# Weight preparation of two bilinear layers asked for in pieces, one per TensorE step, with six staging buffers in the layers before

## The chip, the cores and the metric

The kernel runs on one core of one Trainium2 chip. The metric is the device time of one execution in microseconds. The kernel before was timed three times: 562.81 us in the median, from 562.11 to 563.57 us.

## The reference

Three blocks follow each other. The attention has 2 batches, 8 heads, 768 positions and 64 values a head; each query sees its neighbours at less than 16 positions and one summary per block of 32 keys. Its 1536 x 512 result goes through a maxout layer and through a bilinear layer:

```python
k_sum = k.reshape(B, H, nb, block, D).max(axis=3)
v_sum = v.reshape(B, H, nb, block, D).mean(axis=3)
...
h = np.maximum(np.maximum(x @ w1, x @ w2), x @ w3)     # 512 -> 768
y = h @ w_out                                          # 768 -> 512
...
a = y @ w_a                                            # 512 -> 1536
b = y @ w_b
out = a * b @ w_out                                    # 1536 -> 512
```

## The kernel before, in words

The 1536 tokens are four chunks of 384, two of each batch. Layers one and two are the maxout block, layers three and four the bilinear one. Every matmul with a weight is done three times, since both operands are split into a rounded part and a residual (`mm3`); results gather in PSUM banks.

**Weights.** 60 tiles of 128 x 512 values come as 64-bit numbers, 512 KB each: 24 for layers one and two, 36 for layers three and four. Each goes through three steps. `w_load` is a DMA of SyncE's queue (L421) into a staging buffer. `w_round` makes a float32 of the 64-bit pattern: a scaling on ScalarE or VectorE (L441 or L439), a second one on ScalarE (L443), a shift and a merge on VectorE (L445, L446) and a sum on GpSimd (L447). `w_split` copies on ScalarE (L451) and subtracts on VectorE or GpSimd (L452) to have the rounded part and the residual; in layers three and four all residuals are VectorE's. Layers three's weights are used as 2 x 2 blocks with seven products in place of eight, so `w_split` of a pair also makes four sums of 128 x 256 on VectorE (L467 to L470), splits these two by two, and splits a remaining half.

**Layers three and four.** The order is a0, b0, a1, o0, b1, a2, o1, ... with six of each. A stage a or b is layer three for one slice of 256 of the 1536 columns: seven products for each of two batches, 14 steps of six matmuls. Their banks are called qd, qb and qg. In the first stage of all and in the last b the steps of one batch come before those of the other; elsewhere they alternate. A stage o is layer four, twelve steps of six matmuls of 128 x 512 into banks called po, with two weights. There are 240 steps. After a step, what empties the bank of the step before is issued (`late`, `flush`): ScalarE keeps copies called s, m and u (L624); VectorE adds a kept copy (L634 for an a result called ca, L640 for a b result called t) or multiplies (L638, the last product, t<-qb,ca). A b result of L640 is multiplied by its ca on GpSimd (L641), and each b result is then split by ScalarE (L514) and VectorE (L515) into hg, the input of layer four. VectorE adds the po banks up (L681).

**What sets the order.** Only SyncE's queue runs as written. On the other engines a scheduler plays the program through with durations of its own and sets each queue's order from that, within the data's dependences; where an instruction is issued inside `issue_after(mark)`, it is not placed ahead of that mark. The main loop over `layers34()` asks `weights(2)` after each step. `weights` issues whole weights: it goes on until the slots of split weights are full (`fits`), and slots come free when a stage ends (`w_freed`), so that the work of several weights is asked for at once at the end of a stage and nothing in between.

**Batch one of the attention.** `keys` (L152) loads key rows and `means` (L173) loads transposed values for each of four head pairs; both take their staging buffer from one pool under the name full1, which has `FB[1]` = 2 buffers. From the row, ScalarE copies (L165) and VectorE takes block maxima (L167) and copies them (L168); from the values, VectorE takes block sums (L183). The staging buffers of layers one and two's weights, after the first eight, are `W64[0]` = 4, and `weights` looks six loads ahead at first and two less later, bounded by these buffers.

The functions that the change touches and what calls them, with the line numbers of the profile:

Of the kernel before, what the change touches and what calls it, by code (L numbers as in the profile page):

```python
# [15 lines left out]
ALU = mybir.AluOpType  # L16
# [26 lines left out]
N1, N2, NK = 3 * FF1 // P, FF1 // P, FF2 // P // 3  # L43
N12, N34 = N1 + N2, 9 * NK
# [8 lines left out]

W64, W32, WBUFS, QB, FB, SM, GB, BANKS = (4, 3), (4, 3), (24, 10), 4, (8, 2), 2, (12, 9), (2, 2, 1, 2, 2)

GATE, ROOM, SUMS, EARLY34 = (2, 3), 16, (46, 48, 50, 52), 6
LEAD, TURN, ERA0, ASKS, AHEAD, PRE, TURNS = 5, (11, 2, 2), 8, (3, 4, 5, 7, 9), (4, 1), 3, ((6, N1 - 6, 6, 4, 4, 8, N1 - 8, 4, 12), (24, 34), (34, 44))

# [10 lines left out]
def attention_then_maxout_then_bilinear(ctx: ExitStack, tc: tile.TileContext, qt, kt, vt, vwin, wall, const, out):  # L77
# [4 lines left out]
    V, A, G, T = nc.vector, nc.scalar, nc.gpsimd, nc.tensor  # L82
# [324 lines left out]
    seq = [*range(N12)] + [part(k, 2 * n + i) for k, n, i in kinds[N12:]]  # L407
# [21 lines left out]
    def w_round(q):  # L429


        r = w64_t.pop(q).bitcast(U32).rearrange("p (n t) -> p n t", t=2)
        lw, hw = r[:, :, 0], r[:, :, 1]
        to = hw.bitcast(F32)
        if q < N12 + EARLY34:

            to = ps_c.tile([P, 512], F32, tag="c", name="psw")
        if BIAS_DVE[era(q)][q % 3]:
            V.tensor_scalar(to, hw.bitcast(F32), 2.0 ** -112, None, ALU.mult)  # L439
        else:  # L440
            A.activation(to, hw.bitcast(F32), AF.Copy, scale=2.0 ** -112)  # L441
        hw = to.bitcast(U32)
        A.activation(lw.bitcast(I32), lw, AF.Copy, scale=2.0 ** -29)  # L443
        w32_t[q] = w = w32_p.tile([P, 512], F32, tag=f"w32{q < N12}", name="w32", bufs=W32[q >= N12])
        V.tensor_scalar(w.bitcast(U32), hw, 3, None, ALU.logical_shift_left)  # L445
        V.scalar_tensor_tensor(w.bitcast(U32), hw, 0x80000000, w.bitcast(U32), ALU.bitwise_and, ALU.bitwise_or)  # L446
        G.tensor_tensor(w.bitcast(I32), w.bitcast(I32), lw.bitcast(I32), ALU.add)  # L447

    def w_parts(r, eng, tag="w34", n=512):
        w = w_p.tile([P, 2, n], F32R, tag=tag, name="wt", bufs=2 if n < 512 else WBUFS[tag != "w"])  # L450
        A.activation(w[:, 0], r, AF.Copy)  # L451
        eng.tensor_tensor(w[:, 1], r, w[:, 0], ALU.subtract)  # L452
        return w

    def w_split(q):
        kind, n, i = kinds[q]
        eng = V if SPLIT_DVE[era(q)][q % 3] else G
        if kind in ("w", "o"):
            w_t[q] = w_parts(w32_t.pop(q), eng, "w" if kind == "w" else "w34")
        elif i == 0:  # L460
            w = w_parts(w32_t[q], eng)
            w_t[kind, n] = {"A11": (w, 0), "A12": (w, 256)}
        else:
            w0, w1 = w32_t.pop(q - 1), w32_t.pop(q)
            (a11, a12), (a21, a22) = ((w[:, 0:256], w[:, 256:512]) for w in (w0, w1))
            s12, s34 = (w32_p.tile([P, 512], F32, tag=f"s{i}", name="s", bufs=1) for i in range(2))
            V.tensor_tensor(s12[:, 0:256], a21, a22, ALU.add)  # L467
            V.tensor_tensor(s12[:, 256:512], s12[:, 0:256], a11, ALU.subtract)
            V.tensor_tensor(s34[:, 0:256], a11, a21, ALU.subtract)
            V.tensor_tensor(s34[:, 256:512], a12, s12[:, 256:512], ALU.subtract)  # L470
            s12, s34, a22 = w_parts(s12, eng), w_parts(s34, eng), w_parts(a22, eng, "wb", 256)
            w_t[kind, n].update(S1=(s12, 0), S2=(s12, 256), S3=(s34, 0), S4=(s34, 256), A22=(a22, 0))

    w_at, w_done, w_freed, w_room = [0, 0, 0], 0, 0, 0

    def fits(n):

        return n <= N12 or n - w_freed <= ROOM and n - max(N12, w_freed) <= WBUFS[1]

    def weights(most):  # L480

        nonlocal w_done, w_room
        for _ in range(most):
            if w_done == len(seq) or not fits(w_room + room[w_done]) or w_done == N12 and not gate:
                return
            w_room += room[w_done]
            w_done += 1
            ahead = min(AHEAD[0] + 2 * (w_done < ERA0 + 4), W64[w_done + AHEAD[0] > N12] - 2 * (w_done >= ERA0 + 4))
            for n, (step, more) in enumerate(((w_load, ahead), (w_round, AHEAD[1]), (w_split, 0))):
                while w_at[n] < min(w_done + more, len(seq) if gate else N12):  # L490
                    step(w_at[n])
                    w_at[n] += 1


    late = []
# [107 lines left out]
    def layer3(kind, n, cs):  # L603

        nonlocal w_freed
        ws = w_t[kind, n]
        ps, kept = {}, {}
        each = [(i, b) for i in range(7) for b in range(B)]
        if (kind, n) in (order34[0], order34[-2]):
            each.sort(key=lambda x: x[1])  # L610
        for i, b in each:
            w, y, bank_ = PRODUCTS[i]
            first = (b, bank_) not in ps
            if first:
                ps[b, bank_] = ps_m.tile([P, 512], F32, tag=f"q{bank_}", name=f"q{bank_}")[:, 0:MAXT * P]
            (wt, o), to = ws[w], ps[b, bank_]
            for k in range(2):
                mm3(to, wt, o + k * P, ops[b, y][:, :, k], first and k == 0, k == 1, not first)
            flush()

            def evac(i=i, b=b, to=to):
                def keep(name):
                    kept[b, name] = t = half(name)
                    A.activation(t, to, AF.Copy)  # L624

                def result(f, j, x):

                    c = 2 * b + j
                    if kind == "a":
                        cs[c, f] = t = half("ca")  # L630
                        if x is None:
                            A.activation(t, to, AF.Copy)
                        else:
                            V.tensor_tensor(t, to, x, ALU.add)  # L634
                        return
                    t = half("t")
                    if x is None:
                        V.tensor_tensor(t, to, cs[c, f], ALU.mult)  # L638
                    else:
                        V.tensor_tensor(t, to, x, ALU.add)  # L640
                        G.tensor_tensor(t, t, cs[c, f], ALU.mult)  # L641
                    gs[n, c, f] = g = hg_p.tile([P, 2, MAXT * P], F32R, tag="g", name="hg", bufs=GB[1])
                    split(g, t, V)

                if i in (0, 1, 2):
                    keep(("s1", "m5", "u2")[i])
                elif i == 3:
                    result(0, 0, kept[b, "s1"])
                elif i == 4:
                    result(1, 1, kept[b, "m5"])  # L650
                elif i == 5:
                    result(0, 1, kept[b, "u2"])
                else:
                    result(1, 0, None)

            late.append(evac)
            yield
        w_freed += 3
# [3 lines left out]
    def layer4(n, q):  # L662
        nonlocal w_freed
        for c in range(NCH):
            for i in range(CHUNKS[c][2]):
                ps = bank("po")
                for f in range(2):
                    w, g = w_t[q + f], gs[n, c, f][:, :, i * P:(i + 1) * P]
                    T.matmul(ps, g[:, 0], w[:, 0], start=(f == 0), stop=False)  # L669
                    T.matmul(ps, g[:, 0], w[:, 1], start=False, stop=False)  # L670
                    T.matmul(ps, g[:, 1], w[:, 0], start=False, stop=(f == 1))  # L671
                flush()

                def evac(c=c, i=i, ps=ps):
                    if n == 0:
                        if not acc:
                            sums = acc_p.tile([P, NCH, MAXT, DM], F32, tag="acc", name="acc", bufs=1)
                            acc.update({(c, i): sums[:, c, i] for c in range(NCH) for i in range(MAXT)})
                        A.activation(acc[c, i], ps, AF.Copy)
                    else:  # L680
                        V.tensor_tensor(acc[c, i], ps, acc[c, i], ALU.add)  # L681
                    if n == NG - 1:
                        r0 = (CHUNKS[c][0] * NT + CHUNKS[c][1] + i) * P
                        nc.sync.dma_start(out=out[r0:r0 + P, :], in_=acc[c, i])

                late.append(evac)
                yield
        w_freed += 2
# [48 lines left out]
            done += 1  # L737
    next(dense[-1], None)
    for _ in layers34():
        weights(2)  # L740
    flush()


# [54 lines left out]
```

## Time and profile before

| what | value |
|---|---|
| median of three runs | 562.81 us (562.11 to 563.57) |
| the profiled execution's own time | 561.15 us |
| its span in the profile | 559.3 us |
| mean granted TensorE clock | 0.998 of full speed |
| TensorE busy | 543.4 us, 97% of the span |
| VectorE busy | 376.6 us, 67% |
| ScalarE busy | 278.0 us, 50% |
| GpSimd busy | 200.8 us, 36% |

The span is what the profiler covers of one execution; the execution's own time is 1.85 us longer. PE is TensorE's matmuls, PEld its weight loads, DVE VectorE, ACT ScalarE, POOL GpSimd, SP SyncE. A matmul's end is modelled: twelve matmuls of a row take 2.24 us together, while the mean of one alone is 336 ns, so that one follows the other after (2.24 - 0.336) / 11 = 0.173 us and a gap shown behind a matmul is 0.16 us shorter than the time that TensorE in fact lost. Rows of VectorE that follow each other without a pause overlap by some 0.07 us (298.80 + 0.54 against 299.27).

### The profile page before, as it was taken

What the parts mean: (1) busy time and instruction counts of PE and PEld (TensorE: products, weight loads), DVE (VectorE), ACT (ScalarE), POOL (GpSimd) and SP (SyncE); (2) the same over time, 40 slices, a digit from 0 to 9 for tenths busy, and PEclk for the clock granted to TensorE, in tenths of its full rate; (3) what the DMA queues carried; (4) which work ended last, traced back from release to release, by engine and by line L of the source; (5) the groups of instructions that cost most, each with busy time, mean ns of one, the idle gap of its engine ahead of it and who ended that gap; (6) DMA issues with size and microseconds to landing.
All of it is one profiled execution on the core that took longest, in us unless ns stands there. A gap on an engine that the chain in (4) does not pass through costs nothing.

```text
span 559.3 us, 9056 instructions
## 1 busy us (share of the span) xinstructions
PE 543.4 (97%) x3374; PEld 513.6 (92%) x3374; DVE 376.6 (67%) x781; ACT 278.0 (50%) x667; POOL 200.8 (36%) x177
## 2 busy tenths in 40 slices
PE   8899999999999999999997999999999999999997
PEld 7889999999999999999997899899899989999985
DVE  5798956964433622839869766866977987773374
ACT  4799765666442413525665656534544453341220
POOL 4389996542110111503604322513413332320030
PEclk9999999999999999999999999999999999999999
DMA  8992473833100020312321222122023120000005
GB/s 315 350 269 84 157 249 119 301 113 111 38 1 2 1 97 16 110 42 76 114 75 39 75 77 76 39 76 79 35 76 114 38 77 37 1 0 1 1 32 194
DMA packets 16987, 51.81 MB, mean 93 GB/s; under 512 B 2096, under 2 KB 2480, under 8 KB 16944
## 3 DMA queue, kind: packets, MB, share of 16 engines
q1 hardware_dynamic: 16944, 51.25, 27.4%
q8 instruction: 26, 0.43, 0.3%
q14 instruction: 17, 0.14, 0.1%
HBM read 48.09 MB, written 3.15 MB: 92 GB/s over the span
## 4 chain that ended last, share of the span: by engine, by line
PE 77%; DVE 12%; DMA 4%; ACT 3%; issue 2%; POOL 2%; SPq 0%; POOLq 0%; DVEq 0%; ACTq 0%
PE ph L511 24%; PE qb L511 13%; PE py L511 9%; PE qg L511 5%; PE po L671 5%; PE po L670 5%; PE po L669 5%; PE qd L511 3%; PE ps L250 3%; DVE wt L452 2%; DVE hg L515 2%; DMA w<-wall 2%; PE psv L305 2%; PE pst L286 1%; DVE t L640 1%
## 5 line engine op out<-in xcount | busy, mean ns | idle before, releaser
L511 PE MATMUL ph<-x,wt 128*128 128x384 f32 x864 | 156.2, 336 | 0.1
L511 PEld LDWEIGHTS ph<-x,wt 128*128 128x128 f32 x864 | 149.2, 188 | 0.7 <-DVE x L515 0.5
L447 POOL TENSOR_TENSOR w<-w,w 128x512 int32<-128x512 int32 x60 | 83.0, 1388 | 154.7 <-DVE w L446 78.0
L511 PE MATMUL qb<-yt,wt 128*128 128x384 f32 x576 | 112.9, 336 | 5.5 <-DVE t L640 2.9
L511 PEld LDWEIGHTS qb<-yt,wt 128*128 128x128 f32 x576 | 101.6, 188 | 10.8 <-DVE t L640 3.3
L514 ACT ACTIVATE hg<-t 128x384 fp32r<-128x384 f32 x72 | 37.0, 522 | 81.2 <-DVE t L538 41.5
L641 POOL TENSOR_TENSOR t<-t,ca 128x384 f32<-128x384 f32 x36 | 42.8, 1201 | 85.4 <-DVE t L640 83.0
L681 DVE TENSOR_TENSOR acc<-po,acc 128x512 f32<-128x512 f32 x60 | 40.8, 686 | 27.5 <-PE po L671 27.4
L511 PE MATMUL qg<-yt,wt 128*128 128x384 f32 x288 | 58.0, 336 | 0.5 <-DVE t L640 0.5
L670 PE MATMUL po<-wt,hg 128*128 128x512 f32 x144 | 56.7, 394 | 0.0
L669 PE MATMUL po<-wt,hg 128*128 128x512 f32 x144 | 56.2, 390 | 0.5 <-ACT hg L514 0.5
L671 PE MATMUL po<-wt,hg 128*128 128x512 f32 x144 | 56.2, 396 | 0.2 <-DVE hg L515 0.2
L511 PE MATMUL py<-hg,wt 128*128 128x384 f32 x288 | 55.2, 340 | 0.0
L511 PEld LDWEIGHTS qg<-yt,wt 128*128 128x128 f32 x288 | 50.6, 188 | 2.8 <-DVE t L640 1.0
L538 DVE TENSOR_TENSOR t<-ph,t 128x384 f32<-128x384 f32 x48 | 26.6, 554 | 37.1 <-PE ph L511 31.1
L511 PEld LDWEIGHTS py<-hg,wt 128*128 128x128 f32 x288 | 49.6, 188 | 0.1
L257 ACT ACTIVATE s<-s,nm 128x120 f32<-128x120 f32 x96 | 37.1, 390 | 22.0 <-DVE nm L256 21.3
L451 ACT ACTIVATE wt<-w 128x512 fp32r<-128x512 f32 (+1 forms) x60 | 35.0, 584 | 18.7 <-PE qb L511 12.8
L452 DVE TENSOR_TENSOR wt<-w,wt 128x512 fp32r<-128x512 f32 (+1 forms) x44 | 32.4, 737 | 16.2 <-ACT wt L451 16.2
L515 DVE TENSOR_TENSOR hg<-t,hg 128x384 fp32r<-128x384 f32 x48 | 40.6, 856 | 3.8 <-ACT hg L514 3.8
L515 POOL TENSOR_TENSOR hg<-t,hg 128x384 fp32r<-128x384 f32 x24 | 26.1, 1091 | 46.7 <-ACT hg L514 45.7
L443 ACT ACTIVATE w<-w 128x512 int32<-128x512 uint32 x60 | 39.3, 668 | 0.5 <-DMA w<-wall 0.5
(80 smaller groups left out, 776.7 us busy)
## 6 DMA issues: line engine op xcount, KB each, us to landing
w<-wall SPq DMA_DIRECT2D x60, 512.0 KB, 3.3
q<-qt SPq DMA_DIRECT2D x15, 384.0 KB, 6.7
row<-kt SPq DMA_DIRECT2D x8, 416.0 KB, 5.8
full<-vt SPq DMA_DIRECT2D x8, 384.0 KB, 6.4
out<-acc SPq DMA_DIRECT2D x12, 256.0 KB, 2.0
v<-vwin SPq DMA_DIRECT2D x12, 192.0 KB, 6.7
v<-vwin SPq DMA_DIRECT2D x12, 96.0 KB, 6.8
q<-qt SPq DMA_DIRECT2D x1, 256.0 KB, 4.4
```

Source lines behind the costliest of these rows:

```text
L257: A.activation(s[:, a], s[:, a], AF.Exp, bias=nm[:, a:a + 1], scale=-1.0, accum_out=sm[:, a:a + 1])
L443: A.activation(lw.bitcast(I32), lw, AF.Copy, scale=2.0 ** -29)
L447: G.tensor_tensor(w.bitcast(I32), w.bitcast(I32), lw.bitcast(I32), ALU.add)
L452: eng.tensor_tensor(w[:, 1], r, w[:, 0], ALU.subtract)
L511: T.matmul(ps, w[:, i, o:o + P], x[:, j], start=first and n == 0, stop=last and n == 2, skip_group_check=more)
L514: A.activation(dst[:, 0], src, AF.Copy)
L515: eng.tensor_tensor(dst[:, 1], src, dst[:, 0], ALU.subtract)
L641: G.tensor_tensor(t, t, cs[c, f], ALU.mult)
L669: T.matmul(ps, g[:, 0], w[:, 0], start=(f == 0), stop=False)
L670: T.matmul(ps, g[:, 0], w[:, 1], start=False, stop=False)
L671: T.matmul(ps, g[:, 1], w[:, 0], start=False, stop=(f == 1))
L681: V.tensor_tensor(acc[c, i], ps, acc[c, i], ALU.add)
```

## The change

Three things change.

1. `w_round` and `w_split` become generators that stop two times in a `w_round`, and one time or, for the second weight of a pair, five times in a `w_split`. `work` runs the three steps of a weight as before, `pieces(n)` goes on by n stops, and `weights` runs a whole weight through `pieces`. The loop over layers three and four asks `pieces(1)` after each step instead of `weights(2)`, and issues it inside `issue_after(mark[0])`. `mark[0]`, which layers one and two's `evac` set, is now set by VectorE's evacuations of layers three and four as well. `made` goes on with pieces where a step needs a weight that is not there yet; its loop never runs here.
2. `w_split` of a pair splits its first two sums before it makes the other two.
3. `W64` goes from (4, 3) to (6, 3), so that loads of layers one and two are asked for six ahead at first and four later, and `FB` goes from (8, 2) to (9, 1): one staging buffer in place of two under the name full1.

```diff
-W64, W32, WBUFS, QB, FB, SM, GB, BANKS = (4, 3), (4, 3), (24, 10), 4, (8, 2), 2, (12, 9), (2, 2, 1, 2, 2)
+W64, W32, WBUFS, QB, FB, SM, GB, BANKS = (6, 3), (4, 3), (24, 10), 4, (9, 1), 2, (12, 9), (2, 2, 1, 2, 2)
...
         V.tensor_scalar(w.bitcast(U32), hw, 3, None, ALU.logical_shift_left)
+        yield
         V.scalar_tensor_tensor(w.bitcast(U32), hw, 0x80000000, w.bitcast(U32), ALU.bitwise_and, ALU.bitwise_or)
         G.tensor_tensor(w.bitcast(I32), w.bitcast(I32), lw.bitcast(I32), ALU.add)
+        yield
...
             V.tensor_tensor(s12[:, 0:256], a21, a22, ALU.add)
             V.tensor_tensor(s12[:, 256:512], s12[:, 0:256], a11, ALU.subtract)
+            yield
+            s1 = w_parts(s12, eng)
+            w_t[kind, n].update(S1=(s1, 0), S2=(s1, 256))
+            yield
             V.tensor_tensor(s34[:, 0:256], a11, a21, ALU.subtract)
             V.tensor_tensor(s34[:, 256:512], a12, s12[:, 256:512], ALU.subtract)
-            s12, s34, a22 = w_parts(s12, eng), w_parts(s34, eng), w_parts(a22, eng, "wb", 256)
-            w_t[kind, n].update(S1=(s12, 0), S2=(s12, 256), S3=(s34, 0), S4=(s34, 256), A22=(a22, 0))
+            yield
+            s3 = w_parts(s34, eng)
+            w_t[kind, n].update(S3=(s3, 0), S4=(s3, 256))
+            yield
+            w_t[kind, n].update(A22=(w_parts(a22, eng, "wb", 256), 0))
+            yield
...
+    def work():
+
+        ahead = min(AHEAD[0] + 2 * (w_done < ERA0 + 4), W64[w_done + AHEAD[0] > N12] - 2 * (w_done >= ERA0 + 4))
+        for n, (step, more) in enumerate(((w_load, ahead), (w_round, AHEAD[1]), (w_split, 0))):
+            while w_at[n] < min(w_done + more, len(seq) if gate else N12):
+                w_at[n] += 1
+                yield from step(w_at[n] - 1) or ()
+
+    begun = [iter(())]
+
+    def pieces(most):
...
+        while most:
+            for _ in begun[0]:
+                most -= 1
+                if not most:
+                    return True
             if w_done == len(seq) or not fits(w_room + room[w_done]) or w_done == N12 and not gate:
-                return
+                return False
             w_room += room[w_done]
             w_done += 1
...
+            begun[0] = work()
...
-                            V.tensor_tensor(t, to, x, ALU.add)
+                            mark[0] = V.tensor_tensor(t, to, x, ALU.add).ins
...
-                        V.tensor_tensor(t, to, x, ALU.add)
+                        mark[0] = V.tensor_tensor(t, to, x, ALU.add).ins
...
-                        V.tensor_tensor(acc[c, i], ps, acc[c, i], ALU.add)
+                        mark[0] = V.tensor_tensor(acc[c, i], ps, acc[c, i], ALU.add).ins
...
     for _ in layers34():
-        weights(2)
+        with tc.issue_after(mark[0]):
+            pieces(PIECES)
```

The instructions are the same in kind and number; their order moves. L640 of before is L675 of the changed kernel, L638 is L673, L452 is L454, L446 is L447, L515 is L550, L467, L469, L468 and L470 are L471, L477, L472 and L478.

VectorE at the end of the stage b0, kernel before: qd, qb and qg are banks that it empties, t the result of b, w and s are weights and sums of weights, wt a split weight, hg the split product. The last row is the evacuation of batch one's first qb bank.

```order
L640 TENSOR_TENSOR t<-qd,s_3375 128x384
L640 TENSOR_TENSOR t<-qb,m_3384 128x384
L452 TENSOR_TENSOR wt<-s,wt 128x512
L467 TENSOR_TENSOR s<-w_3534 128x256
L469 TENSOR_TENSOR s<-w_3511,w_3534 128x256
L468 TENSOR_TENSOR s<-s,w_3511 128x256
L452 TENSOR_TENSOR wt<-w_3511,wt 128x512
L470 TENSOR_TENSOR s<-w_3511,s 128x256
L515 TENSOR_TENSOR hg<-t,hg 128x384
L445 TENSOR_SCALAR w_3663<-w_3659 128x512
L515 TENSOR_TENSOR hg<-t,hg 128x384
L640 TENSOR_TENSOR t<-qb,m_3392 128x384
```

VectorE at the same place in the changed kernel, beginning a few weight instructions earlier; its evacuation of that bank is the last row but two.

```order
L447 SCALAR_TENSOR_TENSOR w_3341<-w_3337,w_3341 128x512
L445 TENSOR_SCALAR w_3379<-w_3375 128x512
L454 TENSOR_TENSOR wt<-w_3015,wt 128x256
L447 SCALAR_TENSOR_TENSOR w_3379<-w_3375,w_3379 128x512
L454 TENSOR_TENSOR wt<-w_3341,wt 128x512
L675 TENSOR_TENSOR t<-qd,s_3361 128x384
L675 TENSOR_TENSOR t<-qb,m_3373 128x384
L550 TENSOR_TENSOR hg<-t,hg 128x384 x2
L675 TENSOR_TENSOR t<-qb,m_3387 128x384
L675 TENSOR_TENSOR t<-qg,u_3397 128x384
L675 TENSOR_TENSOR t<-qg,u_3409 128x384
```

Between the two evacuations t<-qb,m stood nine instructions, seven of them on weights; now two stand there, both of hg.

VectorE directly behind that, kernel before, as far as the second t<-qb,ca, which closes b0 (the first row is again the evacuation of qg).

```order
L640 TENSOR_TENSOR t<-qg,u_3409 128x384
L452 TENSOR_TENSOR wt<-s,wt 128x512
L515 TENSOR_TENSOR hg<-t,hg 128x384
L452 TENSOR_TENSOR wt<-w_3352,wt 128x256
L515 TENSOR_TENSOR hg<-t,hg 128x384
L638 TENSOR_TENSOR t<-qb,ca 128x384
L445 TENSOR_SCALAR w_3686<-w_3682 128x512
L638 TENSOR_TENSOR t<-qb,ca 128x384
```

VectorE at the same place in the changed kernel, as far as the first t<-qb,ca.

```order
L471 TENSOR_TENSOR s<-w_3379 128x256
L477 TENSOR_TENSOR s<-w_3341,w_3379 128x256
L447 SCALAR_TENSOR_TENSOR w_3511<-w_3507,w_3511 128x512
L472 TENSOR_TENSOR s<-s,w_3341 128x256
L550 TENSOR_TENSOR hg<-t,hg 128x384
L454 TENSOR_TENSOR wt<-w_3379,wt 128x256
L550 TENSOR_TENSOR hg<-t,hg 128x384
L478 TENSOR_TENSOR s<-w_3341,s 128x256
L673 TENSOR_TENSOR t<-qb,ca 128x384
```

With the shift (L445) of another weight ahead of the first of these rows, nine instructions stand between the last t<-qg,u and the first t<-qb,ca, seven of them on weights; before there were four, two of them on weights.

TensorE at the end of the stage b3, kernel before: po is layer four of the stage o2, which is mixed in; the rows go from b3's last qb products into a4.

```order
L511 MATMUL qb<-yt,wt 128x384 x12
L511 MATMUL qg<-yt,wt 128x384 x12
L511 MATMUL qb<-yt,wt 128x384 x12
L511 MATMUL qg<-yt,wt 128x384 x6
L669 MATMUL po<-wt,hg 128x512
L670 MATMUL po<-wt,hg 128x512
L669 MATMUL po<-wt,hg 128x512
L670 MATMUL po<-wt,hg 128x512
L511 MATMUL qg<-yt,wt 128x384 x6
L671 MATMUL po<-wt,hg 128x512 x2
```

TensorE at the same place in the changed kernel.

```order
L546 MATMUL qb<-yt,wt 128x384 x12
L546 MATMUL qg<-yt,wt 128x384 x18
L546 MATMUL qb<-yt,wt 128x384 x6
L546 MATMUL qg<-yt,wt 128x384 x6
L546 MATMUL qb<-yt,wt 128x384 x6
L705 MATMUL po<-wt,hg 128x512
L706 MATMUL po<-wt,hg 128x512
L705 MATMUL po<-wt,hg 128x512
L706 MATMUL po<-wt,hg 128x512
L707 MATMUL po<-wt,hg 128x512 x2
```

Six matmuls of qg of the next stage now stand ahead of its first qb: the step that needs the qb bank, emptied by t<-qb,ca, comes six matmuls later, and the two qb steps are apart.

On SyncE's queue, two loads of weights that stood between the loads of batch one's head pairs now stand ahead of the first of them, 15 in a row in place of 13.

## Rows read from the trace of the kernel before

**Rows 1.** The page's first lines: the span, and TensorE's and the other engines' busy time.

```profile
span 559.3 us, 9056 instructions
PE 543.4 (97%) x3374; PEld 513.6 (92%) x3374; DVE 376.6 (67%) x781; ACT 278.0 (50%) x667; POOL 200.8 (36%) x177
```

**Rows 2.** Busy time of each engine by window: start:end, length, then busy (instructions), clock, DMA.

```profile
70.00:280.00 210.00, 210.00 (x1407) 206.89 (x1407) 120.28 (x274) 102.20 (x253) 74.18 (x62) 1.00 0.28 93
300.00:310.00 10.00, 7.04 (x39) 6.36 (x38) 10.00 (x15) 6.88 (x14) 6.62 (x6) 1.00 0.15 54
```

**Rows 3.** TensorE's waits from 285 to 559 us: total us, times, longest us.

```profile
PE qb L511 <- DVE t L640: 2.9, 1, 2.9
PE qb L511 <- DVE t L638: 2.0, 4, 0.9
PE qb L511 <- ACT u L624: 0.6, 1, 0.6
PE qg L511 <- DVE t L640: 0.5, 1, 0.5
PE po L669 <- ACT hg L514: 0.5, 1, 0.5
PE po L671 <- DVE hg L515: 0.2, 1, 0.2
```

**Rows 4.** TensorE's timeline at b0's end: start us, us, what [idle before <-releaser].

```profile
301.01 2.24 PE L511 MATMUL qb<-yt,wt 128*128 128x384 f32 x12
306.20 1.33 PE L511 MATMUL qb<-yt,wt 128*128 128x384 f32 x6 [2.95 <-DVE t L640]
307.37 4.63 PE L511 MATMUL qg<-yt,wt 128*128 128x384 f32 x24
312.94 2.35 PE L511 MATMUL qb<-yt,wt 128*128 128x384 f32 x12 [0.95 <-DVE t L638]
```

**Rows 5.** VectorE's timeline at the same place.

```profile
298.80 0.54 DVE L640 TENSOR_TENSOR t<-qd,s 128x384 f32<-128x384 f32 x1
299.27 0.54 DVE L640 TENSOR_TENSOR t<-qb,m 128x384 f32<-128x384 f32 x1
...
305.60 0.55 DVE L640 TENSOR_TENSOR t<-qb,m 128x384 f32<-128x384 f32 x1
...
306.53 1.25 DVE L446 SCALAR_TENSOR_TENSOR w<-w,w 128x512 uint32<-128x512 uint32 x1
...
311.88 0.54 DVE L515 TENSOR_TENSOR hg<-t,hg 128x384 fp32r<-128x384 f32 x1
...
313.61 0.68 DVE L446 SCALAR_TENSOR_TENSOR w<-w,w 128x512 uint32<-128x512 uint32 x1
```

**Rows 6.** VectorE's sums of line 469: minimum/median/maximum ns of one, first and last start.

```profile
L469 DVE TENSOR_TENSOR s<-w,w x12: 411/418/1243, 229.8 to 472.1; 128x256 f32<-128x256 f32 x12
```

**Rows 7.** The page's costliest groups: count | busy, mean ns of one | idle before.

```profile
L447 POOL TENSOR_TENSOR w<-w,w 128x512 int32<-128x512 int32 x60 | 83.0, 1388 | 154.7 <-DVE w L446 78.0
...
L514 ACT ACTIVATE hg<-t 128x384 fp32r<-128x384 f32 x72 | 37.0, 522 | 81.2 <-DVE t L538 41.5
L641 POOL TENSOR_TENSOR t<-t,ca 128x384 f32<-128x384 f32 x36 | 42.8, 1201 | 85.4 <-DVE t L640 83.0
...
L451 ACT ACTIVATE wt<-w 128x512 fp32r<-128x512 f32 (+1 forms) x60 | 35.0, 584 | 18.7 <-PE qb L511 12.8
```

**Rows 8.** TensorE's waits from 40 to 72 us.

```profile
PEld ph L511 <- DVE x L515: 0.5, 1, 0.5
```

**Rows 9.** SyncE's queue, the second row of batch one.

```profile
98.59 0.33 SPq L152 DMA_DIRECT2D row<-kt  x1
```

**Rows 10.** VectorE's timeline where batch one's rows are consumed.

```profile
98.38 0.94 DVE L183 TENSOR_REDUCE mean<-full 128x24 f32<-128x768 f32 x1
...
101.85 0.95 DVE L167 TENSOR_REDUCE top<-row 128x24 f32<-128x768 f32 x1 [0.51 <-DMA row<-kt]
```

**Rows 11.** VectorE's waits from 285 to 540 us.

```profile
DVE wt L452 <- ACT wt L451: 20.4, 13, 3.7
```

More of the change, by code (lines that the diff above doesn't have):

```diff
@@ L52 @@
             ("S4", "B22", "g"), ("A22", "T4", "b"))
-W64, W32, WBUFS, QB, FB, SM, GB, BANKS = (4, 3), (4, 3), (24, 10), 4, (8, 2), 2, (12, 9), (2, 2, 1, 2, 2)
+W64, W32, WBUFS, QB, FB, SM, GB, BANKS = (6, 3), (4, 3), (24, 10), 4, (9, 1), 2, (12, 9), (2, 2, 1, 2, 2)
 GATE, ROOM, SUMS, EARLY34 = (2, 3), 16, (46, 48, 50, 52), 6
-LEAD, TURN, ERA0, ASKS, AHEAD, PRE, TURNS = 5, (11, 2, 2), 8, (3, 4, 5, 7, 9), (4, 1), 3, ((6, N1 - 6, 6, 4, 4, 8, N1 - 8, 4, 12), (24, 34), (34, 44))
+PIECES, LEAD, TURN, ERA0, ASKS, AHEAD, PRE, TURNS = 1, 5, (11, 2, 2), 8, (3, 4, 5, 7, 9), (4, 1), 3, ((6, N1 - 6, 6, 4, 4, 8, N1 - 8, 4, 12), (24, 34), (34, 44))
 EARLY, BIAS_DVE, SPLIT_DVE = 16, ((0, 1, 0), (0, 1, 0), (0, 0, 0)), ((0, 0, 1), (0, 0, 1), (1, 1, 1))
@@ L468, in w_split @@
             V.tensor_tensor(s12[:, 256:512], s12[:, 0:256], a11, ALU.subtract)
+            yield
+            s1 = w_parts(s12, eng)
+            w_t[kind, n].update(S1=(s1, 0), S2=(s1, 256))
+            yield
             V.tensor_tensor(s34[:, 0:256], a11, a21, ALU.subtract)
             V.tensor_tensor(s34[:, 256:512], a12, s12[:, 256:512], ALU.subtract)
-            s12, s34, a22 = w_parts(s12, eng), w_parts(s34, eng), w_parts(a22, eng, "wb", 256)
-            w_t[kind, n].update(S1=(s12, 0), S2=(s12, 256), S3=(s34, 0), S4=(s34, 256), A22=(a22, 0))
+            yield
+            s3 = w_parts(s34, eng)
+            w_t[kind, n].update(S3=(s3, 0), S4=(s3, 256))
+            yield
+            w_t[kind, n].update(A22=(w_parts(a22, eng, "wb", 256), 0))
+            yield
     w_at, w_done, w_freed, w_room = [0, 0, 0], 0, 0, 0
@@ L478, in fits, with weights, made @@
         return n <= N12 or n - w_freed <= ROOM and n - max(N12, w_freed) <= WBUFS[1]
-    def weights(most):
-        nonlocal w_done, w_room
-        for _ in range(most):
+    def work():
[6 more added lines that the diff above has]
+    def pieces(most):
+        nonlocal w_done, w_room
+        while most:
[3 more added lines that the diff above has]
+                    return True
             if w_done == len(seq) or not fits(w_room + room[w_done]) or w_done == N12 and not gate:
-                return
+                return False
             w_room += room[w_done]
             w_done += 1
[L488 to L492, printed above, removed]
+            begun[0] = work()
+    def weights(most):
+        for _ in range(most):
+            if not pieces(1):
+                return
+            for _ in begun[0]:
+                pass
+    def made(kind, n, tile_):
+        while not (tile_ in w_t.get((kind, n), ()) if kind in "ab" else n in w_t):
+            assert pieces(1)
     late = []
@@ L605, in layer3 @@
         nonlocal w_freed
-        ws = w_t[kind, n]
         ps, kept = {}, {}
@@ L615, in layer3 @@
                 ps[b, bank_] = ps_m.tile([P, 512], F32, tag=f"q{bank_}", name=f"q{bank_}")[:, 0:MAXT * P]
-            (wt, o), to = ws[w], ps[b, bank_]
+            made(kind, n, w)
+            (wt, o), to = w_t[kind, n][w], ps[b, bank_]
             for k in range(2):
@@ L667, in layer4 @@
                 for f in range(2):
+                    made("o", q + f, None)
                     w, g = w_t[q + f], gs[n, c, f][:, :, i * P:(i + 1) * P]
```

## The prediction

> **What bounds the kernel now.** The page's first lines come first: TensorE is busy for 543.4 of 559.3 us [rows 1]. The windows come second. From 70 to 280 us, layers one and two, it has 210.00 us of work in 210 [rows 2]: nothing can be won there, only lost. What the change can win lies in layers three and four, and so TensorE's waits from 285 to 559 us are the third view. They are few: 2.9 us for t<-qb,m (L640), 2.0 us in four waits for t<-qb,ca (L638), 0.6 us for a copy of ScalarE, 0.5 us for L640 again, 0.5 and 0.2 us for hg [rows 3]. That is 6.7 us, and all but the 0.6 hang on VectorE or on the split of hg.
>
> The fourth view is the place of the longest wait, at the end of b0. Between 300 and 310 us VectorE is busy for 10.00 of 10 us and TensorE for 7.04 [rows 2]. TensorE's last qb products before the gap end at 303.25 (301.01 + 2.24), and it goes on at 306.20 [rows 4]; VectorE empties that bank at 305.60 [rows 5]. VectorE could have done so from 303.25 on, 2.35 us sooner, had it not been working through nine queued instructions that follow the evacuation at 299.27, seven of them on weights of later stages. The second wait, 0.95 us at 312.94 [rows 4], is the same thing one step on.
>
> **The change part by part.** Counts and kinds of instructions stay, so the sum is one of waits. It is made on the profiled execution, 561.15 us (its span of 559.3 and 1.85 us around it); the median shown is 562.81, 1.66 us more, and the forecast is moved by that.
>
> *A, the wait of 2.95 us.* In the changed order only two hg subtractions stand between the two t<-qb,m. They need a product of GpSimd and a copy of ScalarE each. t<-qd ends at 299.34 [rows 5]; two products of 1.20 us and a copy of 0.52 [rows 7] give 302.3, and the second subtraction of 0.54 [rows 5] is done by some 302.9, ahead of 303.25. The evacuation is then late only by its own length: 2.95 becomes 0.6, -2.35 us. If the bank were free ahead of the products, 0.4 more; if two GpSimd sums of weights (1.388 us each [rows 7]) stood ahead of the two products, the hg would be done at 305.7, a loss of 0.3. Bounds -2.75 and +0.3; I take -2.35, since the row's times put the hg ahead of the bank.
>
> *B, the wait of 0.95 us for t<-qb,ca.* The weight work has to go somewhere, and here it is: nine instructions now stand between the last t<-qg,u and t<-qb,ca where four stood. From the moment when t<-qb,m lets TensorE go on, TensorE has 30 matmuls, at 0.173 us each 5.2 us [rows 4]. VectorE has two evacuations of 0.55, six short weight instructions of 0.42 [rows 6], a merge of 0.68, two hg of 0.54 and the evacuation itself: 1.1 + 2.5 + 0.7 + 1.1 + 0.55 = 5.9, less 0.07 of overlap for each of twelve, 5.1 us. So at best it just fits (-0.95, and 0.16 of modelled end). At worst each of the seven weight instructions is stretched, as L469's longest to 1.24 [rows 6] and the merge to 1.25 [rows 5]: 0.82 x 6 + 0.57 = 5.5 more, a wait of 5.4, +4.5. I take two of the seven stretched, since the median of L469 is 0.418 and only its tail is long: 5.1 + 1.6 - 5.2 = 1.5 us, +0.6.
>
> *C, D, E, the smaller waits.* The 0.2 us for hg goes with A (-0.2; bounds -0.2 and +0.5, the nearest wait for hg). In b1 to b3 there are four waits: t<-qb,ca three times, 1.03 us (2.0 less B's 0.95), and t<-qg,u once, 0.5 [rows 3]. In the changed order more of TensorE's work stands ahead of the qb bank that it waits for, as the six matmuls of qg at b3's end (1.04 us, more than any of the four), and the evacuations of qg follow those of qb directly. I take 1.55 to 0.2, -1.35; bounds -1.55, and +1.0 if one new wait as long as the present 0.95 comes. The 0.5 us for ScalarE's copy of hg late in b5 [rows 3]: the copies of weights are done by then in the changed order, -0.5; bounds -0.5 and 0. The 0.6 us ahead of b0 waits for a copy of ScalarE, which the change does not touch: 0.
>
> *F, modelled ends.* A matmul alone shows 0.336 us but the next can follow after 0.173, so each wait that vanishes gives 0.16 more than its row shows. Four do (C, E and two of D): -0.65.
>
> *G, staging of six.* Two loads of weights come sooner. The one wait behind a late weight is 0.5 us of PEld for x at about 65 us [rows 8], behind a chain that begins with a load: -0.3, bounds -0.5 and 0.
>
> *H, one staging buffer for batch one.* The wait for a buffer stands on SyncE's queue, and behind it the q and v loads of the same head pair and all later ones; VectorE's maxima and, through the scores, TensorE wait for these. Before, the second row is issued at 98.59 [rows 9], as soon as the first row's maximum is done, and the next maximum still waits 0.51 us for it [rows 10]: this load has no slack. In the changed kernel it waits for the sum of the values too, 0.94 us [rows 10]. TensorE has layers one and two to do meanwhile and no gap there [rows 2], so some is covered. Between 0 and 0.9 I take +0.5.
>
> Sum: -2.35 + 0.6 - 0.2 - 1.35 - 0.5 - 0.65 - 0.3 + 0.5 = -4.25. On the profiled execution 561.15 becomes 556.9; on the median 562.81 becomes 558.6.
>
> **A rule that speaks against it.** L469 takes 0.411 us at the least and 1.243 at the most for one shape [rows 6], and the merge 0.68 and 1.25; the evacuations stay at 0.54 or 0.55 [rows 5]. The Trainium skill, page "SBUF — State Buffer", section "Who interferes with whom", says that VectorE and GpSimd share a pair of ports as an exclusive lock, that VectorE instructions with two SBUF inputs are among those held up, and that those with one are not; the trace agrees in these numbers, since the evacuations read one operand from PSUM. By that rule the change puts B's weight instructions beside GpSimd's products by ca, which B's sum prices at two stretched instructions; the rule at its strictest is the first rival.
>
> **The rivals.**
> *R1, the stall moves rather than goes.* Three products of 1.20 us [rows 7] hold VectorE up for 3.6 us in B's stretch instead of 1.6: the wait there is 5.1 + 3.6 - 5.2 = 3.5, +2.55 instead of +0.6, and the same mechanism keeps D's 1.35. -4.25 + 1.95 + 1.35 = -0.95: 561.9. For it speaks that VectorE has no free time in this window [rows 2], against it that L469's median is the short one.
> *R2, the one buffer stalls the attention of batch one.* Each of the seven loads behind the first waits for the consumer of the one before it, 0.94 us each [rows 10]: 6.6 instead of 0.5, 564.7. For it speaks the present wait of 0.51 [rows 10], against it that TensorE is without a gap [rows 2].
> *R3, a queue's head waits: the other side.* A piece per step issues a weight's merge, GpSimd's sum (1.388), ScalarE's copy (0.584) [rows 7] and VectorE's residual a step or two apart. VectorE works in order; in the changed order the residual of w_3341 comes, with 1.3 to 1.5 us of work between, behind a chain of 1.97: it waits some 0.6, and the evacuations t<-qd and t<-qb,m stand right behind it. Ten stages have such a place; if each costs TensorE 0.7 us, that is 7 us: 565.6. It decides from six places on (6 x 0.7 = 4.2). Against it: VectorE already waits 20.4 us in 13 places for the copy L451 [rows 11], one of 3.7 us, and TensorE's waits are still only 6.7 us [rows 3], because it has other work in its queue.
> *R4, nothing.* The order moves but the waits stay what they are: 562.8.
>
> **How the numbers follow.** What a measurement of this kernel can tell from no change is about 0.3%, 1.7 us: below 561.1 is faster, above 564.5 slower. Forecast 0.60 (558.6; its own range 556 to 561, from B at its short end with D at its best to A half kept); R1 0.13, R2 0.08, R3 0.14, R4 0.05. Nearly all of the forecast, and a little of R1, is faster, 0.60; R1's rest, half of R2 and R4 are no change, 0.21; R3 and the other half of R2 are slower, 0.19. The best ends of A to G together give some -7.5, 555.3, the low end; the high end of 564.7 takes in R1, R2 and R4 and leaves R3 out, as the case with the highest price.
>
> **What would show it.** Right: among TensorE's waits from 285 us on the one of 2.9 us for t<-qb,m is under 0.8, one for t<-qb,ca in b0 lies between 0.5 and 2, all together under 4 us; between 300 and 310 us TensorE is busy for over 9 us; from 70 to 280 us it stays at 210. Wrong for A: t<-qb,m still over 2 us late, with GpSimd's sums ahead of its products. R1: t<-qb,ca over 3 us, with L469 and the merge at 1.24 around it. R2: TensorE below 207 us from 70 to 280, VectorE waiting for row or full. R3: new waits of TensorE for L675 or L673 right behind a residual L454 that waits for ScalarE, in six stages or more. The time is off with the steps right if waits come in banks that have none now, the po banks above all, since VectorE's weight work now lies evenly over all steps.

## The result: 566.18 us, 0.68% slower

The changed kernel takes 566.18 us in the median of four runs (565.60 to 567.31), the kernel before 562.70 beside it: a ratio of 1.0068, 95% interval 1.0055 to 1.0081. The forecast was 558.6, the range ended at 564.7. Between the two profiled executions, 561.15 and 566.29 us, the difference is 5.1 us, since that of before is one of its quicker ones; the trace of after accounts for 5.0 of them.

The page of after begins so:

```profile
span 564.5 us, 8995 instructions
PE 545.7 (97%) x3374; PEld 516.5 (91%) x3374; DVE 372.4 (66%) x781; ACT 279.4 (49%) x667; POOL 200.5 (36%) x177
```

TensorE still counts as busy for 97%, with 2.3 us more of it than in [rows 1] for the same matmuls; 1.5 us of that are matmuls that ran slower, as shown below. The same two windows as in [rows 2]:

```profile
70.00:280.00 210.00, 210.00 (x1409) 206.92 (x1408) 116.82 (x269) 102.27 (x254) 73.34 (x61) 1.00 0.25 83
300.00:310.00 10.00, 8.37 (x46) 7.41 (x44) 7.78 (x13) 6.28 (x14) 7.28 (x7) 1.00 0.30 107
```

Layers one and two lose nothing, and b0's end has won: TensorE is busy for 8.37 us where it was 7.04. What has come in its place shows in TensorE's waits from 285 us on (total, times, longest), to be read beside [rows 3]:

```profile
PE qb L546 <- DVE t L673: 5.7, 4, 2.6
PE qg L546 <- ACT m L659: 3.0, 3, 1.6
PE qb L546 <- DVE t L675: 0.7, 1, 0.7
PE qb L546 <- ACT u L659: 0.6, 1, 0.6
```

L675 is L640 of before, L673 is L638, L659 is ScalarE's copies L624. The wait of 2.9 us for t<-qb,m is 0.7, those for hg are gone, but t<-qb,ca takes 5.7 in place of 2.0, and copies called m, which nobody waited for, 3.0.

Counted from one matmul's start to the next, less the usual 0.173 us (0.231 for po), all that TensorE loses from 280 us on is 9.5 us before and 14.5 after, +5.0. By place: the wait for t<-qb,m of b0 3.2 to 1.0; t<-qb,ca of b0 1.2 to 0.7; m in b0 none to 1.9; b1 to b4 2.7 to 9.8; the two waits for hg 1.2 to none. The loss is in b2, b3 and b4; b0 as a whole has won 0.8.

**b4.** TensorE's longest wait, with VectorE and GpSimd at that time (start us, us, what):

```profile
503.67 1.31 PE L546 MATMUL qb<-yt,wt 128*128 128x384 f32 x6 [2.58 <-DVE t L673]
```

```profile
496.28 1.24 DVE L445 TENSOR_SCALAR w<-w 128x512 uint32<-128x512 uint32 x1
497.44 2.11 DVE L447 SCALAR_TENSOR_TENSOR w<-w,w 128x512 uint32<-128x512 uint32 x2
499.46 3.68 DVE L550 TENSOR_TENSOR hg<-t,hg 128x384 fp32r<-128x384 f32 x3
503.07 1.01 DVE L673 TENSOR_TENSOR t<-qb,ca 128x384 f32<-128x384 f32 x2
```

```profile
494.79 3.61 POOL L676 TENSOR_TENSOR t<-t,ca 128x384 f32<-128x384 f32 x3 [1.50 <-DVE t L675]
499.17 3.09 POOL L448 TENSOR_TENSOR w<-w,w 128x512 int32<-128x512 int32 x2 [0.78 <-ACT hg L549]
```

VectorE is never idle here. A shift (L445) and two merges of weights, the pieces of two steps, come ahead of the three hg. Beside GpSimd's three products by ca, which run to 498.40, the shift takes 1.24 us where the median of these shifts is 0.42, and the merges take 2.11 in place of 1.3 (0.68 each in [rows 5], less 0.07 of overlap). The merges release two sums of GpSimd, and beside these the three hg take 3.68 us in place of some 1.5 (0.54 each in [rows 5], less 0.07 of overlap twice). t<-qb,ca waits behind all of it.

**b3.** Here ScalarE is late first, then VectorE.

```profile
449.59 0.40 ACT L453 ACTIVATE wt<-w 128x256 fp32r<-128x256 f32 x1
449.94 0.67 ACT L441 ACTIVATE w<-w 128x512 f32<-128x512 f32 x1
450.51 0.66 ACT L443 ACTIVATE w<-w 128x512 int32<-128x512 uint32 x1
451.06 0.51 ACT L549 ACTIVATE hg<-t 128x384 fp32r<-128x384 f32 x1
451.47 0.48 ACT L659 ACTIVATE m<-qg 128x384 f32<-128x384 f32 x1
```

```profile
452.00 1.34 PE L546 MATMUL qg<-yt,wt 128*128 128x384 f32 x6 [1.59 <-ACT m L659]
454.41 2.29 PE L546 MATMUL qb<-yt,wt 128*128 128x384 f32 x6 [1.07 <-DVE t L673]
```

Three weight instructions stand on ScalarE ahead of m, without a pause. The six matmuls behind 454.41 take 2.29 us, and those at 452.00, just ahead of them, 1.34. The windows around it (length, TensorE busy, ..., granted clock) say why:

```profile
450.00:455.00 5.00, 2.34 (x11) 1.69 (x10) 5.00 (x9) 3.57 (x8) 2.02 (x2) 0.94 0.08 18
455.00:460.00 5.00, 5.00 (x22) 4.87 (x21) 3.62 (x9) 3.50 (x7) 0.00 (x0) 0.72 0.23 90
460.00:465.00 5.00, 5.00 (x29) 4.84 (x28) 3.15 (x6) 1.50 (x3) 1.30 (x1) 1.00 0.27 94
```

After the two waits TensorE is granted the lower of its two levels (1.2 in place of 2.4 GHz) for some 3 us: matmuls follow each other after 0.320 us in place of 0.173, which costs 1.5 us more. That is part of b3's loss, not another cause. In most executions of the kernel before, the mean granted clock is as low as in the changed kernel's (0.994 to 0.997 in 13 of the 17 timed beside mark_all, 0.993 to 0.996 in the changed kernel's four), but 0.998 in the profiled one; between the medians, which lie 3.5 us apart, this part therefore counts for less.

### The profile page after: what moved, and what is told of

Read it like the earlier page. It is cut to its first block, busy times and chain, and to the rows that moved or that the text cites. A ratio compares the mean times of both kernels' runs of the same rounds, so it can differ in the third digit from the quotient of the medians.

```text
span 564.5 us, 8995 instructions
## 1 busy us (share of the span) xinstructions
PE 545.7 (97%) x3374; PEld 516.5 (91%) x3374; DVE 372.4 (66%) x781; ACT 279.4 (49%) x667; POOL 200.5 (36%) x177
## 4 chain that ended last, share of the span: by engine, by line
PE 83%; DVE 8%; DMA 3%; ACT 2%; issue 2%; POOL 1%; SPq 0%; ACTq 0%
PE ph L546 27%; PE qb L546 15%; PE py L546 9%; PE qg L546 6%; PE po L707 5%; PE po L706 5%; PE po L705 5%; PE qd L546 3%; PE ps L250 3%; DVE hg L550 2%; PE psv L305 2%; PE pst L286 2%; DMA full<-vt 1%; DMA q<-qt 1%; DVE w L447 1%
## 5 line engine op out<-in xcount | busy, mean ns | idle before, releaser
L546 PE MATMUL qb<-yt,wt 128*128 128x384 f32 x576 | 116.4, 339 | 7.1 <-DVE t L673 5.7
L546 PE MATMUL qg<-yt,wt 128*128 128x384 f32 x288 | 59.9, 339 | 3.0 <-ACT m L659 3.0
L676 POOL TENSOR_TENSOR t<-t,ca 128x384 f32<-128x384 f32 x36 | 41.0, 1156 | 49.0 <-DVE t L675 44.7
L550 POOL TENSOR_TENSOR hg<-t,hg 128x384 fp32r<-128x384 f32 x24 | 26.6, 1112 | 47.7 <-ACT hg L549 47.7
L550 DVE TENSOR_TENSOR hg<-t,hg 128x384 fp32r<-128x384 f32 x48 | 34.7, 735 | 9.4 <-ACT hg L549 9.2
L275 POOL TENSOR_TENSOR s<-s,r 128x720 f32<-128x720 f32 x16 | 22.3, 1392 | 44.7 <-DVE r L273 32.4
```

The lines of the kernel that those rows point to most:

```text
L546: T.matmul(ps, w[:, i, o:o + P], x[:, j], start=first and n == 0, stop=last and n == 2, skip_group_check=more)
L550: eng.tensor_tensor(dst[:, 1], src, dst[:, 0], ALU.subtract)
```

## The experiments

Each kernel was timed in five rounds beside the kernel before, which took 562.41 to 563.03 us in these groups; the ratios are to that.

### mark_all: the mark at t<-qb,ca too

```diff
-                        V.tensor_tensor(t, to, cs[c, f], ALU.mult)
+                        mark[0] = V.tensor_tensor(t, to, cs[c, f], ALU.mult).ins
```

> The changed kernel, with the mark set by the evacuation t<-qb,ca (L673) too, so that pieces asked for after it are not placed ahead of it. Theory 'place' (in the changed kernel weight pieces stand on VectorE between the last t<-qg,u and t<-qb,ca, and TensorE waits there): TensorE's waits for L673 fall from 5.7 to under 1 us, those for ScalarE's m from 3.0 to under 1, the stretch at half clock behind 454 us is gone, 556 to 560 us. Theory 'port' (VectorE is late there because GpSimd's products and sums hold it up, whatever stands there): the hg subtractions stay beside the products and are late still, 562 to 565 us. Theory 'staging' (the buffers cost the time): no change, 565 to 567 us.

Measured: 559.09 us, ratio 0.9935 (0.9923 to 0.9948). One line turns +0.68% into -0.65%. TensorE's waits from 285 us on:

```profile
PE qb L546 <- ACT u L659: 2.5, 2, 1.9
PE qb L546 <- DVE t L675: 0.7, 1, 0.7
PE qd L546 <- DVE t L675: 0.6, 1, 0.6
PE qb L546 <- ACT s L659: 0.3, 1, 0.3
```

None for L673 and none for m: theory 'place' holds, and 'staging' falls, as staging is that of the changed kernel. The scheduler also ordered TensorE's queue anew (in b3 the last twelve qb matmuls now stand together, with three po matmuls ahead of them), and what that gave by itself is not shown. The expectation missed one thing, a new wait of 1.88 us at 458 us, on ScalarE, with a stretch at the lower clock behind it (granted clock 0.76 from 460 to 465 us):

```profile
456.38 0.67 ACT L441 ACTIVATE w<-w 128x512 f32<-128x512 f32 x1 [2.72 <-DMA w<-wall]
456.95 0.65 ACT L443 ACTIVATE w<-w 128x512 int32<-128x512 uint32 x1
457.50 0.85 ACT L659 ACTIVATE u<-qb 128x384 f32<-128x384 f32 x2
```

```profile
458.02 1.49 PE L546 MATMUL qb<-yt,wt 128*128 128x384 f32 x6 [1.88 <-ACT u L659]
```

The head of ScalarE's queue waits 2.72 us for a weight to land, and the copy u that TensorE needs stands two instructions behind it.

### mark_all_old_staging: the same with W64 (4, 3) and FB (8, 2)

```diff
-W64, W32, WBUFS, QB, FB, SM, GB, BANKS = (6, 3), (4, 3), (24, 10), 4, (9, 1), 2, (12, 9), (2, 2, 1, 2, 2)
+W64, W32, WBUFS, QB, FB, SM, GB, BANKS = (4, 3), (4, 3), (24, 10), 4, (8, 2), 2, (12, 9), (2, 2, 1, 2, 2)
```

> As mark_all, with the staging of the kernel before, W64 (4, 3) and FB (8, 2). Theories 'place' and 'port': within 0.7 us of mark_all, as the order in layers three and four is the same. Theory 'staging': 3 to 5 us under mark_all, and TensorE's waits in layers three and four the same in both.

Measured: 558.45 us, ratio 0.9931 (0.9917 to 0.9944), within the interval of mark_all. The staging buffers, six or four, one or two, are worth nothing that shows.

### no_mark: pieces without the mark

```diff
     for _ in layers34():
-        with tc.issue_after(mark[0]):
-            pieces(PIECES)
+        pieces(PIECES)
```

With the staging of before.

> Pieces one per step, but without the mark around them, and with the staging of the kernel before. In the order the nine instructions, seven on weights, stand between b0's two t<-qb,m again, and two to four ahead of t<-qb,ca. Theory 'place': the wait for t<-qb,m is back at 2 to 3 us, those for t<-qb,ca at 1 to 3 us in all, 561 to 564 us. Rival 'pace' (work spread evenly over the steps costs by itself, through queue heads that wait for GpSimd and ScalarE): 565 to 567 us, as the changed kernel.

Measured: 562.53 us, ratio 1.0007 (0.9997 to 1.0017), no change. The waits are those of [rows 3] again:

```profile
PE qb L546 <- DVE t L675: 3.1, 1, 3.1
PE qb L546 <- DVE t L673: 1.7, 3, 1.2
PE qg L546 <- DVE t L675: 0.9, 1, 0.9
```

So the pieces alone neither win nor lose, and, as the staging is worth nothing, it is the mark that removed b0's long wait. In the changed kernel the mark held weight work behind t<-qb,m and t<-qg,u, and not behind t<-qb,ca: the work that it pushed out came to stand there.

### products_on_dve_b2_on: the products by ca on VectorE

```diff
-                        G.tensor_tensor(t, t, cs[c, f], ALU.mult)
+                        (V if n > 1 else G).tensor_tensor(t, t, cs[c, f], ALU.mult)
```

The rest is the changed kernel.

> The changed kernel with the products by ca of the slices 2 to 5 on VectorE in place of GpSimd; the order up to the end of b1 is unchanged, and ahead of t<-qb,ca stand as many weight instructions as before plus up to three products. Theory 'port': no instruction of VectorE there is stretched any more, TensorE's waits in b2 to b4 (6.9 us in the changed kernel) fall under 2 us, 559 to 562 us. Theory 'place': VectorE's queue ahead of t<-qb,ca is longer than before, the waits stay at 5 us or more, 565 to 569 us.

Measured: 558.49 us, ratio 0.9933 (0.9921 to 0.9945). The waits:

```profile
PE qg L546 <- ACT m L659: 1.9, 2, 1.6
PE qb L546 <- DVE t L673: 1.9, 2, 1.5
PE qb L546 <- DVE t L675: 0.7, 1, 0.7
PE qb L546 <- ACT u L659: 0.6, 1, 0.6
```

From b2 on 6.9 us of waits became about 2 (1.5 for L673 in b2, some 0.4 for m in b3; the rest is b0's, where no product was moved), and the time at the lower clock is gone, though VectorE has more to do. So 'place' as first put is not enough: weight work ahead of t<-qb,ca costs what it does because of what GpSimd has to do beside it. Either cure removes the loss. Not all of the 5 us is shown to be the stretch alone, for three more things moved. The scheduler placed the weight work somewhat differently from b2 on; it ordered TensorE's queue anew (in b4, fifteen more matmuls stand ahead of the last qb steps); and ScalarE's hg copies, two of which wait 1.51 and 0.63 us for products in b3 of the changed kernel and stand ahead of m, no longer depend on GpSimd. The sums of weights stayed on GpSimd, and VectorE is still stretched beside them: its own L471 takes 1.53 us at 401 us, in b2, beside one of GpSimd's that begins at 400.73, ahead of the wait that is left.

### mark_all_whole and mark_all_two: is it the pace?

```diff
-            pieces(PIECES)
+            weights(2)
```

This is mark_all_whole; mark_all_two is mark_all with PIECES = 2.

> The kernel mark_all with weights(2) in place of pieces(1) inside the mark: whole weights in bursts, but never ahead of VectorE's last evacuation. Theory 'mark' (what mattered is which evacuations the weight work stays behind, not how it is cut): within 1 us of mark_all, 557.5 to 560 us, no wait of TensorE for L673 over 0.5 us. Rival 'pace' (the even spread brings the gain): a burst behind a mark holds the evacuations after it up as in the kernel before, 561 to 564 us.

> The kernel mark_all with two pieces per step. Theory 'mark': 557.5 to 560 us. Rival 'pace': between mark_all and the kernel before, 560 to 562 us.

Measured: 555.81 us, ratio 0.9886 (0.9872 to 0.9900), and 556.62 us, 0.9900 (0.9887 to 0.9912). Both lie under every range that was stated. The condition of 'mark' holds, as no wait for L673 is left, and 'pace' falls the other way round: pieces of one step are the slowest of the three. The wait at 458 us is in neither; what TensorE loses from 280 us on is 4.2 and 4.9 us, beside 7.4 in mark_all. That one wait, 2.1 us from start to start, and the 1.6 us of slower matmuls behind it are more than the whole difference, so the runs do not show that pace by itself costs anything.

### mark_all_products and whole_products: do the two cures add up?

mark_all, and mark_all_whole, each with the products of the slices 2 to 5 on VectorE.

> The kernel mark_all with the products by ca of the slices 2 to 5 on VectorE. Theory 'place times port' (weight work ahead of t<-qb,ca costs because GpSimd's products stretch it): with the weight work gone from there nothing is left for the move to win; the wait for ScalarE's u at 456 us, which hangs on a load, stays: 557.5 to 560 us. Rival 'the two gains add': 553 to 556 us.

> mark_all_whole with the products by ca of the slices 2 to 5 on VectorE. Theory 'place times port': mark_all_whole has no wait for L673 left and one late wait of 0.5 us for hg, so 554.5 to 556.5 us, at most the 0.7 us of that wait under it. Rival 'the two gains add': under 554 us.

Measured: 556.00 us, 0.9890 (0.9874 to 0.9906), and 556.16 us, 0.9883 (0.9859 to 0.9907). The first is 3.1 us better than mark_all, at the upper end of what 'the two gains add' had: the wait of 1.88 us for u is not there any more, and no run says whether it went by the freed GpSimd or by another order. The second adds nothing to mark_all_whole, as 'place times port' had it. From the changed kernel's 566.18 us one cure takes 7.1 us, the other 7.7, and both together 10.2, not 14.8: they add only in part, and nothing here goes much under 556.

### before_products: the kernel before with all products on VectorE

> The kernel before with all products by ca on VectorE. Theory 'port': the nine instructions between b0's two t<-qb,m took 6.3 us because five are stretched by 0.4 to 0.8 us each; unstretched, and with the products of 0.55 among them, the wait of 2.95 us falls to about 2, that of 0.95 to 0.3, the waits in b1 to b3 fall too: 559 to 561 us. Rival 'place': as many instructions and more stand ahead of the evacuations: 562 to 565 us.

Measured: 561.35 us, ratio 0.9986 (0.9971 to 1.0002): at best 0.3%, and undecided between the two theories. The wait for t<-qb,m is 1.9 us in place of 2.9, as expected, but two others of 1.9 and 1.2 us (from 280 us on) came elsewhere, for copies of ScalarE.

### before_marks: the kernel before with the mark alone

```diff
-                            V.tensor_tensor(t, to, x, ALU.add)
+                            mark[0] = V.tensor_tensor(t, to, x, ALU.add).ins
...
-                        V.tensor_tensor(t, to, cs[c, f], ALU.mult)
+                        mark[0] = V.tensor_tensor(t, to, cs[c, f], ALU.mult).ins
...
-        weights(2)
+        with tc.issue_after(mark[0]):
+            weights(2)
```

L640 and L681 set the mark likewise; no pieces, staging as before.

> The kernel before, with nothing but the mark: set by VectorE's evacuations of layers three and four, t<-qb,ca among them, and put around weights(2). No pieces, staging as before. Theory 'mark': as mark_all_whole, 555 to 557 us, TensorE's waits from 285 us on at 2 to 3.5 us. Rival 'the generators matter' (the splitting of the first two sums ahead of the other two, or the staging): over 558 us.

Measured: 556.08 us, ratio 0.9877 (0.9857 to 0.9896): theory 'mark' holds. TensorE's waits from 285 us on are all in these rows, 2.1 us where [rows 3] have 6.7:

```profile
PE qb L511 <- DVE t L640: 1.0, 1, 1.0
PE qb L511 <- ACT u L624: 0.6, 1, 0.6
PE po L669 <- ACT hg L514: 0.5, 1, 0.5
```

Five places in the kernel before, and no generator, give what the best of the others gives. This and mark_all_whole beat both kernels: the one before by 1.2 and 1.1%, the changed one, by the medians, by 1.8%.

## Why the prediction was wrong, step by step

*A* held: 2.95 to 0.74 us against a forecast of 0.6, by the mechanism given; two hg stand between the evacuations. TensorE's rows at b0's end, for *A* and *B*, and VectorE's:

```profile
304.40 1.31 PE L546 MATMUL qb<-yt,wt 128*128 128x384 f32 x6 [0.74 <-DVE t L675]
...
308.60 1.32 PE L546 MATMUL qg<-yt,wt 128*128 128x384 f32 x6 [0.80 <-ACT m L659]
310.49 1.32 PE L546 MATMUL qg<-yt,wt 128*128 128x384 f32 x6 [0.57 <-ACT m L659]
312.22 1.31 PE L546 MATMUL qb<-yt,wt 128*128 128x384 f32 x6 [0.42 <-DVE t L673]
```

```profile
302.62 1.25 DVE L550 TENSOR_TENSOR hg<-t,hg 128x384 fp32r<-128x384 f32 x2 [2.09 <-ACT hg L549]
303.79 0.55 DVE L675 TENSOR_TENSOR t<-qb,m 128x384 f32<-128x384 f32 x1
...
305.64 1.24 DVE L471 TENSOR_TENSOR s<-w 128x256 f32<-128x256 f32 x1
306.81 1.23 DVE L477 TENSOR_TENSOR s<-w,w 128x256 f32<-128x256 f32 x1
...
308.90 1.66 DVE L550 TENSOR_TENSOR hg<-t,hg 128x384 fp32r<-128x384 f32 x1
...
311.62 0.55 DVE L673 TENSOR_TENSOR t<-qb,ca 128x384 f32<-128x384 f32 x1
```

*B* was to grow from 0.95 to 1.5 us and shrank to 0.42, though the stretch was if anything underrated: two sums at 1.24 and 1.23 as taken, and an hg of 1.66 on top. TensorE was held back sooner, by two waits of 0.80 and 0.57 us for m in b0, which gave t<-qb,ca time. The three together are 1.79 us, so the size of *B* came out near the forecast by luck, mostly through another engine; the two waits for m also kept TensorE at 8.37 us between 300 and 310, under the 9 that was named as a sign. The first m starts at 308.07 on ScalarE, five instructions behind a weight's scaling that had waited for VectorE's shift:

```profile
305.81 0.66 ACT L441 ACTIVATE w<-w 128x512 f32<-128x512 f32 x1 [2.52 <-DVE w L445]
```

Between them stand two more weight instructions and two hg copies. No term of the sum asked what ScalarE has ahead of its evacuations.

*C and E* held; both waits for hg are gone.

*D is the step that failed.* It read TensorE's order and said that with more work ahead of the qb bank the four waits of 1.55 us would fall to 0.2. It never counted what VectorE's queue holds ahead of t<-qb,ca in b1 to b4, as B did for b0. In b4 four weight and three hg instructions stand between the last t<-qg,u and the first t<-qb,ca, where the kernel before has two of each. The waits are 1.62 us in b2, 1.59 (for m) and 1.07 in b3 and 2.58 in b4, 6.9 in all where 0.2 was forecast, and 1.5 us at the lower clock, for which there was no term. The upper bound of D, +1.0, was one wait as long as the present one; a bound made as B's was, +4.5 for one stage, would have shown that a loss of this size could come. From start to start b1 to b4 went up by 7.1 us where the forecast took 1.35 off: over 8 of the 9.3 us between the forecast's -4.25 and the 5.0 that came.

*F* is real but small. *G and H*: the wait of 0.5 us of [rows 8] is gone, and VectorE waits longer for the second row than in [rows 10], 1.76 us in place of 0.51, 1.25 more, where 0.9 was the bound, since its issue slips from 98.59 to 102.33:

```profile
105.51 0.95 DVE L167 TENSOR_REDUCE top<-row 128x24 f32<-128x768 f32 x1 [1.76 <-DMA row<-kt]
```

TensorE covers it all, as the 210.00 us above show, and mark_all_old_staging confirms it. *R2* is out.

*R1 had the mechanism and the name of the wait* but was priced for b0 alone and kept D's waits as they were, which is why it ended at no change. The Trainium skill, page "SBUF — State Buffer", section "Who interferes with whom", has the rule that VectorE's instructions with two SBUF inputs contend with GpSimd's that read SBUF; the trace agrees in b4 (three hg in 3.68 us beside two sums), and with the products off GpSimd most of the loss goes. The prediction weighed the rule at one place of five. It also put the exemption of one SBUF input too widely: the page leaves VectorE's two-port modes out of it, and the shift L445, with one input, takes 1.24 us in b4 above and up to 1.54 in the trace of before, where its median is 0.42.

*R3* is wrong for VectorE. Its waits for ScalarE's copy of a weight, 20.4 us in [rows 11], are fewer:

```profile
DVE wt L454 <- ACT wt L453: 3.5, 4, 1.1
```

A queue's head that waits did cost TensorE time, but on ScalarE: in b0 of the changed kernel, for VectorE's shift (the 2.52 us above), and in mark_all, for a load (the 2.72 us above). The side of 0.19 came out, by a case that was counted as no change.

## What to carry to other kernels

In this kernel, background work that the scheduler may place was best held behind every instruction of VectorE that frees a bank; the fence that left one out sent the work there. ScalarE's copies, which free banks too, were in no fence, and that was not tried. Count what each engine's queue holds ahead of each evacuation, at every stage and on the copying engine too, and price it at its stretched length where the two engines that hinder each other both work. Spreading work evenly was worth nothing by itself here (no_mark), and once the fence was right it was 3.3 us worse than bursts (mark_all against mark_all_whole), which the one wait behind a load accounts for.

## What the runs showed of the hardware

**Either engine can be the one held up.** In the changed kernel's b4 three hg took 3.68 us beside two sums of GpSimd, which took 3.09, 0.3 more than the 2 x 1.39 of [rows 7]. In mark_all's b3 three hg take 1.48 us, while a sum on GpSimd takes 3.62 in place of 1.39:

```profile
449.39 1.48 DVE L550 TENSOR_TENSOR hg<-t,hg 128x384 fp32r<-128x384 f32 x3
```

```profile
449.36 3.62 POOL L448 TENSOR_TENSOR w<-w,w 128x512 int32<-128x512 int32 x1 [2.23 <-DVE w L447]
```

The operations and shapes are the same, and in both places VectorE had an instruction under way when the sum began. What decides which of the two waits was not tried.

**A short wait can cost twice.** The lower clock came after waits of 1.59 and 1.07 us with six matmuls between (the changed kernel, 455 us) and after one of 1.88 us (mark_all, 458 us), and not after one of 2.58 us (the changed kernel, 504 us) or, in the profiled execution of the kernel before, of 2.95 us [rows 4]. In no_mark it came after nearly the same wait, at the same place:

```profile
306.72 2.29 PE L546 MATMUL qb<-yt,wt 128*128 128x384 f32 x6 [3.07 <-DVE t L675]
```

The length of the wait alone does not decide it, and one kernel can go either way: the mean granted clock is 0.997 in four executions of mark_all (559.05 to 559.34 us) and 1.000 in the fifth (557.69 us). What tells these apart was not found.
